# Cosine-gated MLP behind linear attention on one Trainium2 core: the second layer's product with seven half-size products instead of eight

## The chip, the cores and the metric

The kernel runs on one core of one Trainium2 chip. The metric is the device time of one execution in microseconds. Before the change the median of 3 runs is 312.84 us (312.84 to 312.94).

## The reference

The inputs are q, k and v of 8 batches, 8 heads, 576 positions and 64 values a head (float32), w_in (512 x 2048) and w_out (2048 x 512). Attention is linear: no softmax, but features phi and two products, normalised by a sum.

```
c, s = cos(pi/2 * pos/576), sin(pi/2 * pos/576)
phi(x) = concat(relu(x) * c, relu(x) * s)            # 64 -> 128 features
q_p, k_p = phi(q), phi(k)
kv  = k_p^T @ v            # per batch and head, 128 x 64
z   = sum of k_p over positions
num = q_p @ kv ;  den = q_p . z + 1e-6
attn = num / den
x = attn as (8*576 tokens, 512)
h = x @ w_in               # first layer, 4608 x 2048
g = h * cos(h)
out = g @ w_out            # second layer, 4608 x 512
```

## The kernel before

All products run in f16 with sums in float32. The 4608 tokens are cut into nine chunks of 512 (`SM`): chunks 0 to 7 are the first 512 positions' worth of a batch, and chunk 8 (`xR`) gathers the 64 tokens that each batch has left over. `NJT` = 16 is the number of 128-row blocks of the inner dimension 2048, `NCT` = 4 that of 512.

For a batch, `attention(b)` loads k, q and v, forms phi on DVE and ACT (`prep`, lines 235 and 238), casts v into `V1` (`cast_v`, two buffers, with a column of ones that makes z come out of the same product), forms kv on PE (`kv`, line 259), transposes q (`q_pe` on PE in the early batches, `q_dma` on the DMA queue later), forms numerator and denominator (`num`, lines 322 to 342) and transposes the normalised result (`x_pe` or `x_dma`) into `xT`.

`layer1(c)` makes h transposed, 128 inner values by 512 tokens at a time: 4 matmuls of 512 columns into one of three PSUM banks `M1` (line 425), or, for chunks 0 and 1, 8 matmuls of 256 columns (line 408). `gate` then takes cos on ACT as a sine with a bias (line 381), and DVE multiplies it with h into `gT` (line 383), which is f16, inner blocks by tokens, with two buffers for alternate chunks.

`layer2(c)` uses `gT` as the stationary operand: for each of four blocks of 128 tokens, 16 matmuls of 512 columns accumulate over the inner dimension into one of two banks `M2` (line 449). ACT copies the bank to `ost` (line 461; the last one is split between ACT and DVE, lines 464 and 467), and SP's queue stores it (line 472). In the steady part `layer2(c-1)` runs beside `layer1(c)`.

The order of the work is written by a planner (`Plan`). Each step names its engine, its assumed time, a due time, and the keys that it reads and writes. `run` simulates the five queues: at each point it takes, among all steps that are ready, the one that can start first, and of equal ones the one with the earlier due time, and this fixes every engine's program order. Due times come from `start[c]` and `width[c]`; periods are `TP` = 30 us apart in the planner's time. The engines then run their own lists in order and wait for each other by semaphores. Weights come over POOL's queue (lines 514 and 524), and the loads of batch 1 wait for a part of w_out (`hold_raw`, line 528).

Of the kernel before, what the change touches and what calls it, by code (L numbers as in the profile page):

```python
# [99 lines left out]
def kernel(  # L100
# [9 lines left out]
    nc = tc.nc  # L110
# [71 lines left out]
    pl = Plan()  # L182
    MM, MMH, MMA, MMT = 0.2157, 0.109, 0.031, 0.057

    T0, TW, TP = 17.0, 46.0, 30.0
    start = [T0, TW] + [TW + 14.0 + TP * n for n in range(NC)]
    width = [14.0, 14.0] + [TP] * NC

# [51 lines left out]
                op0=ALU.max, op1=ALU.mult), rd, wr)  # L240

    def cast_v(b, t, eng, due, hs=slice(0, H)):
        out_, in_ = V1[b % 2][:, t, hs, 0:D], raw["v"][:, hs, t, :]
        heads = range(H)[hs]
        rd, wr = hk("v", heads), [("V1", b % 2, t, h) for h in heads]
        f = len(heads) / H
        if eng == "ACT":
            act(0.2 + 0.37 * f, due, lambda: nc.scalar.activation(
                out=out_, in_=in_, func=AF.Copy), rd, wr)
        else:  # L250
            dve(0.09 + 0.28 * f, due, lambda: nc.vector.tensor_copy(  # L251
                out=out_, in_=in_), rd, wr)

    def kv(b, due, split=False):
        def mm(hb):
            for hh in range(HB):
                h = hb * HB + hh
                for t in range(NT + 1):
                    nc.tensor.matmul(  # L259
                        ATT[:, hb, hh * D1:(hh + 1) * D1],  # L260
                        lhsT=kp[:, t, h].rearrange("p g d -> p (g d)"),
                        rhs=V1[b % 2][:, t, h, :], start=(t == 0), stop=(t == NT))
        for hb in range(2):
            hs = range(hb * HB, (hb + 1) * HB)
            pe(HB * (NT + 1), MMA, due, lambda hb=hb: mm(hb),
               [("kp", t, g, h) for t in range(NT + 1) for g in range(2) for h in hs]
               + [("V1", b % 2, t, h) for t in range(NT + 1) for h in hs],
               [("ATT", hb)])
# [119 lines left out]
    def layer1(c):  # L388
        X = xT[c % 2] if c < B else xR
        xk = [("xT", c % 2, t) for t in range(NT)] if c < B else [("xR", i) for i in range(NT)]  # L390
        G = gT[c % 2]
        if c < 2:
            n = 0
            for quarter in range(4):
                for hf in range(2):
                    for jp in range(2):
                        j0 = quarter * 4 + jp * 2
                        m = m1n[0] % NM1
                        m1n[0] += 1
                        due = start[c] + n * width[c] / NJT  # L400
                        n += 1
                        ts = slice(hf * 2 * P, (hf + 1) * 2 * P)

                        def mm(m=m, j0=j0, ts=ts):
                            for jj in range(2):
                                j = j0 + jj
                                for cc in range(NCT):
                                    nc.tensor.matmul(  # L408
                                        M1[m][:, jj * 2 * P:(jj + 1) * 2 * P],
                                        lhsT=w_in_sb[:, cc, j * P:(j + 1) * P], rhs=X[:, cc, ts],  # L410
                                        start=(cc == 0), stop=(cc == NCT - 1))
                        pe(2 * NCT, MMH, due, mm, xk[2 * hf:2 * hf + 2] + [("w_in", quarter)],
                           [("M1", m)])
                        gate(M1[m], ("M1", m), G[:, j0:j0 + 2, ts],
                             [("g", c, j, t) for j in (j0, j0 + 1) for t in (2 * hf, 2 * hf + 1)],
                             due + 1.5)
            return
        for j in range(NJT):
            m = m1n[0] % NM1
            m1n[0] += 1  # L420
            due = start[c] + j * width[c] / NJT

            def mm(m=m, j=j):
                for cc in range(NCT):
                    nc.tensor.matmul(M1[m], lhsT=w_in_sb[:, cc, j * P:(j + 1) * P], rhs=X[:, cc, :],  # L425
                                     start=(cc == 0), stop=(cc == NCT - 1))
            pe(NCT, MM, due, mm, xk + [("w_in", j // 4)], [("M1", m)])
            gate(M1[m], ("M1", m), G[:, j, :], [("g", c % 2, j, t) for t in range(NT)], due + 1.5)
# [5 lines left out]

    on = [0]

    def layer2(c):
        G = gT[c % 2]
        NQ = 4
        for t in range(NT):  # L440
            m = m2n[0] % NM2
            m2n[0] += 1
            w0, ww = (start[c + 1], width[c + 1]) if 0 < c < B else (start[c] + width[c], 14.0)
            for jq in range(NQ):
                due = w0 + ((t + (jq + 1) / NQ) / NT) * ww * 0.97

                def mm(m=m, t=t, jq=jq):
                    for j in range(jq * NJT // NQ, (jq + 1) * NJT // NQ):
# [5 lines left out]
            last = c == NC - 1 and t == NT - 1  # L454
            if t % 2 == 0:
                o = on[0] % NO
                on[0] += 1
            O = ost[o]
            due += 1.0
            if not last:  # L460
                act(0.5, due, lambda O=O, t=t, m=m: nc.scalar.activation(  # L461
                    out=O[:, t % 2, :], in_=M2[m], func=AF.Copy), [("M2", m)], [("ost", o, t % 2, 0)])
            else:
                act(0.3, due, lambda O=O, t=t, m=m: nc.scalar.activation(
                    out=O[:, t % 2, 0:256], in_=M2[m][:, 0:256], func=AF.Copy),
                    [("M2", m)], [("ost", o, t % 2, 0)])
                dve(0.33, due, lambda O=O, t=t, m=m: nc.vector.tensor_copy(
                    out=O[:, t % 2, 256:512], in_=M2[m][:, 256:512]),
                    [("M2", m)], [("ost", o, t % 2, 1)])

            def put(dst, s, keys, q=nc.sync, eng="SP", nb=256.0):
                pl.add(eng, 0.65, 0, due + 1.0, lambda: q.dma_start(out=dst, in_=s), keys, [],
                       dma=(nb, 330.0))
            if c < B:
                if t % 2 == 1:
                    n = c % 2
                    five, four = rows(c)
                    keys = [("ost", o, 0, 0), ("ost", o, 1, 0)]
                    put(five[:, t - 1:t + 1, :], blocks(O, n), keys)
                    put(four[:, t - 1:t + 1, :], blocks(O, 1 - n), keys)  # L480
            else:
                for n in range(2):
                    five, _ = rows(2 * t + n)
                    if not last:
                        put(five[:, NT, :], blocks(O, n)[:, t % 2], [("ost", o, t % 2, 0)], nb=131.0)
                    else:
                        for f in range(2):
                            fs = slice(f * 256, (f + 1) * 256)
                            put(five[:, NT, fs], blocks(O, n)[:, t % 2, fs],
                                [("ost", o, t % 2, f)], *((nc.scalar, "ACT") if f == 0 else (nc.sync, "SP")), nb=65.0)  # L490


    def setup():
        for nm in "kqv":
            nc.vector.memset(raw[nm][:, :, NT, :], 0.0)
        nc.vector.memset(PIH, math.pi / 2.0)
        nc.scalar.dma_start(out=CS, in_=cs_dr.ap())
        nc.scalar.dma_start(out=IDENT, in_=ident_dr.ap())
        nc.scalar.activation(out=WARM, in_=PIH, func=AF.Sin)
        for n in range(2):  # L500
            nc.gpsimd.memset(V1[n][:, :, :, D], 1.0)

    wi = moe_w_in.rearrange("(c p) f -> p c f", p=P)
    wo = moe_w_out.rearrange("(j p) m -> p j m", p=P)
# [144 lines left out]
```

## Time and profile before

| what | value |
|---|---|
| median of 3 runs | 312.84 us (312.84 to 312.94) |
| the profiled execution's own time | 311.55 us |
| its span, first to last instruction | 309.8 us |
| busy: PE, DVE, ACT | 284.9, 183.0, 185.9 us |
| weight loads on PE (beside the matmuls) | 158.2 us, 2092 of them |
| moved by DMA | 51.91 MB |
| mean granted TensorE clock | 0.994 |

An engine's busy time is the time that it had an instruction in work. Matmuls are pipelined: each one's recorded length is a latency, and what a stream of them costs is told by the distance of their starts. PEld is the weight loads, which run beside the matmuls. In the groups of instructions a row reads line, engine, operation, output<-input, shapes, count | busy us, mean ns of one | idle time of the engine just before them and who ended it. In the order of time a row reads start, length (both in us), engine, line and so on, with the idle time ahead of it in brackets. In the windows, each engine's busy time and count follow the length of the window, then the granted clock, the DMA share and GB/s.

### The profile page before, as it was taken

How to read it: one execution, taken by the hardware profiler on the slowest of the kernel's cores; microseconds unless marked ns; L12 is line 12 of the kernel's file. 1: busy time of each engine (PE TensorE's matmuls, PEld its weight loads, DVE VectorE, ACT ScalarE, POOL GpSimd, SP SyncE). 2: the span in 40 equal slices, each digit the busy share in tenths (PEclk: the TensorE clock that was granted, in tenths of full speed). 3: DMA queues.
4: the chain of work that ended last, by engine and by line, in shares of the span. 5: the costliest groups of instructions: out<-in, count | busy, mean ns of one | idle time of the engine just before them, and what ended most of it. 6: DMA issues, size and time to landing. Idle time of an engine off the chain costs nothing.

```text
span 309.8 us, 5467 instructions
## 1 busy us (share of the span) xinstructions
PE 284.9 (92%) x2092; PEld 158.2 (51%) x2092; DVE 183.0 (59%) x402; ACT 185.9 (60%) x297; POOL 7.9 (3%) x19
## 2 busy tenths in 40 slices
PE   0468999689999999999999999999999999999994
PEld 0447856477864555455545554544444444444441
DVE  1667655979896973985587665733565434343300
ACT  1947759689986856944884586444544454555311
POOL 0331000000000000000000000000000000000000
PEclk9999999989999999999999999999999999999999
DMA  6899998995499998997999732960132010101121
GB/s 195 271 210 223 187 324 270 357 332 164 142 234 232 364 177 218 309 268 118 282 341 252 119 102 65 159 148 5 69 70 85 1 70 0 69 0 70 42 94 68
DMA packets 72218, 51.91 MB, mean 168 GB/s; under 512 B 40832, under 2 KB 69760, under 8 KB 72192
## 3 DMA queue, kind: packets, MB, share of 16 engines
q1 hardware_dynamic: 67520, 47.20, 55.8%
q0 software_dynamic: 4224, 4.19, 8.3%
q8 instruction: 16, 0.26, 0.3%
q10 hardware_dynamic: 448, 0.17, 0.2%
q14 instruction: 10, 0.08, 0.1%
HBM read 36.74 MB, written 9.44 MB: 149 GB/s over the span
## 4 chain that ended last, share of the span: by engine, by line
PE 85%; DVE 5%; ACT 4%; DMA 2%; issue 1%; SPq 0%; DVEq 0%; ACTq 0%
PE M L449 39%; PE M L425 31%; PE M L408 7%; PE ATT L259 3%; PE ATT L322 3%; DMA qm<-in_q_dram 2%; DVE x L342 2%; PE M L290 1%; ACT ch L381 1%; ACT kp L235 1%; ACT qp L235 1%; DVE V L251 1%; DVE qp L238 1%; PE TR L290 0%; PE TR L361 0%
## 5 line engine op out<-in xcount | busy, mean ns | idle before, releaser
L381 ACT ACTIVATE ch<-M,PIH 128x512 f32<-128x512 f32 x144 | 98.5, 692 | 80.4 <-PE M L425 60.6
L383 DVE TENSOR_TENSOR gT<-M,ch 128x512 f16<-128x512 f32 x144 | 98.3, 687 | 77.3 <-ACT ch L381 76.8
L449 PE MATMUL M<-w_out_sb,gT 128*128 128x512 f16 x576 | 142.6, 379 | 0.0
L425 PE MATMUL M<-xT,w_in_sb 128*128 128x512 f16 x384 | 96.9, 379 | 0.0
L449 PEld LDWEIGHTS <-gT 128*128 128x128 f16 x576 | 54.5, 98 | 60.5
L425 PEld LDWEIGHTS <-w_in_sb 128*128 128x128 f16 x448 | 43.3, 98 | 51.1
L408 PE MATMUL M<-xT,w_in_sb 128*128 128x256 f16 x256 | 30.2, 272 | 0.7 <-ACT xT L365 0.7
L235 ACT ACTIVATE kp<-km,CS 128x512 f16<-128x512 f32 x40 | 26.5, 719 | 6.5 <-DMA km<-in_k_dram 6.5
L461 ACT ACTIVATE ost<-M 128x512 f32<-128x512 f32 x35 | 20.7, 594 | 15.5 <-PE M L449 15.1
L235 ACT ACTIVATE qp<-qm,CS 128x512 f16<-128x512 f32 x39 | 26.4, 726 | 2.9 <-DMA qm<-in_q_dram 2.7
L408 PEld LDWEIGHTS <-w_in_sb 128*128 128x128 f16 x256 | 24.4, 98 | 3.6 <-issue 0.8
L238 DVE TENSOR_SCALAR kp<-km,CS 128x512 f16<-128x512 f32 x40 | 16.9, 480 | 14.3 <-DMA km<-in_k_dram 11.1
L342 DVE TENSOR_TENSOR x<-ATT,rec 128x512 f16<-128x512 f32 x30 | 20.6, 688 | 0.8
L238 DVE TENSOR_SCALAR qp<-qm,CS 128x512 f16<-128x512 f32 x41 | 18.3, 477 | 2.5 <-DMA qm<-in_q_dram 2.5
L322 PEld LDWEIGHTS <-qT 128*128 128x128 f16 x320 | 14.3, 98 | 6.7 <-issue 1.0
L290 PEld LDWEIGHTS <-qp 128*128 128x128 f16 x120 | 8.9, 111 | 15.2 <-ACT qp L235 12.2
L425 PE MATMUL M<-xR,w_in_sb 128*128 128x512 f16 x64 | 16.4, 379 | 0.0
L290 PE MATMUL M<-IDENT,qp 128*128 128x128 f16 x56 | 4.9, 259 | 12.2 <-ACT qp L235 12.2
L259 PE MATMUL ATT<-V,kp 128*128 128x65 f16 x320 | 13.3, 202 | 2.5 <-DVE x L342 1.7
L259 PEld LDWEIGHTS <-kp 128*128 128x128 f16 x320 | 12.6, 103 | 5.2 <-issue 2.7
L251 DVE CAST V<-vm 128x512 f16<-128x512 f32 (+1 forms) x42 | 14.0, 383 | 0.0
L322 PE MATMUL ATT<-kvz,qT 128*128 128x65 f16 x272 | 13.5, 194 | 0.0
(43 smaller groups left out, 76.6 us busy)
## 6 DMA issues: line engine op xcount, KB each, us to landing
out_dram<-ost SPq DMA_DIRECT2D x32, 256.0 KB, 2.6
km<-in_k_dram SPq DMA_DIRECT2D x8, 640.0 KB, 5.3
qm<-in_q_dram SPq DMA_DIRECT2D x8, 640.0 KB, 5.2
km<-in_k_dram SPq DMA_DIRECT2D x8, 512.0 KB, 6.2
qm<-in_q_dram SPq DMA_DIRECT2D x8, 512.0 KB, 6.2
vm<-in_v_dram SPq DMA_DIRECT2D x6, 640.0 KB, 7.1
vm<-in_v_dram SPq DMA_DIRECT2D x6, 512.0 KB, 7.7
w_in_sb<-in_moe_w_in_dram POOLq DMA_DIRECT2D x4, 512.0 KB, 9.4
```

Source lines behind the costliest of these rows:

```text
L235: act(0.2 + 0.37 * f, due, lambda: nc.scalar.activation(out=out_, in_=in_, func=AF.Relu, scale=sc), rd, wr)
L238: dve(0.09 + 0.28 * f, due, lambda: nc.vector.tensor_scalar(out=out_, in0=in_, scalar1=0.0, scalar2=sc, op0=ALU.max, op1=ALU.mult), rd, wr)
L251: dve(0.09 + 0.28 * f, due, lambda: nc.vector.tensor_copy(out=out_, in_=in_), rd, wr)
L259: nc.tensor.matmul(ATT[:, hb, hh * D1:(hh + 1) * D1], lhsT=kp[:, t, h].rearrange("p g d -> p (g d)"), rhs=V1[b % 2][:, t, h, :], start=(t ...
L322: nc.tensor.matmul(bank[hb][:, hh * D1:(hh + 1) * D1], lhsT=a[:, h, :], rhs=z[:, h, :], start=(i == 0), stop=(i == len(parts) - 1))
L342: dve(0.08 + 0.27 * k, due, lambda A=A, hs=hs, k=k: nc.vector.tensor_tensor(out=split(x16[n][:, hs, :], k), in0=A[:, :, :, 0:D], in1=split ...
L381: act(0.59, due, lambda: nc.scalar.activation(out=ch[c], in_=bank, func=AF.Sin, bias=PIH, scale=1.0), [key, "PIH"], [("ch", c)])
L383: dve(0.61, due, lambda: nc.vector.tensor_tensor(out=dst, in0=bank if len(dst.shape) == 2 else bank.rearrange("p (j s) -> p j s", j=dst.sh ...
L408: nc.tensor.matmul(M1[m][:, jj * 2 * P:(jj + 1) * 2 * P], lhsT=w_in_sb[:, cc, j * P:(j + 1) * P], rhs=X[:, cc, ts], start=(cc == 0), stop= ...
L425: nc.tensor.matmul(M1[m], lhsT=w_in_sb[:, cc, j * P:(j + 1) * P], rhs=X[:, cc, :], start=(cc == 0), stop=(cc == NCT - 1))
L449: nc.tensor.matmul(M2[m], lhsT=G[:, j, t * P:(t + 1) * P], rhs=w_out_sb[:, j, :], start=(j == 0), stop=(j == NJT - 1))
L461: act(0.5, due, lambda O=O, t=t, m=m: nc.scalar.activation(out=O[:, t % 2, :], in_=M2[m], func=AF.Copy), [("M2", m)], [("ost", o, t % 2, 0)])
```

## The change

The second layer of chunks 1 to 8 is done with one level of Strassen's scheme (Winograd's form: seven products). The operands are cut in halves: `gT` by tokens (`TH` = 256) and by inner blocks (`JH` = 8), `w_out` by inner blocks and by columns (`MH` = 256). With a11, a12, a21, a22 for `gT` (first index tokens, second inner half) and b11 to b22 for `w_out`, the sums and products are:

```
T1 = b12 - b11   T3 = b22 - b12   T2 = b22 - T1   T4 = b21 - T2      # once, w_out_sums
S3 = a11 - a21   S1 = a21 + a22 (in a21's place)   S2 = S1 - a11   S4 = a12 - S2 (in a12's place)
bank A : a11 b11 -> copy Y1 ; + S2 T2 -> copy U2 ; + S3 T3 -> c22 = bank + Z5 ; + a22 T4 -> c21
bank Bk: a12 b21 -> c11 = bank + Y1 ; new: S1 T1 -> copy Z5 ; + S4 b22 -> c12 = bank + U2
```

The products are issued in the order A, Bk, A, Bk, A, Bk, A. Each is 2 token blocks x 8 inner blocks of matmuls with 256 columns. Sums of `gT` are made on DVE in f16, in two halves of four inner blocks each; the four copies are on ACT, the three adds that end an output quarter on DVE. `layer1` now alternates between the two inner halves, so that the first halves of the sums can be made before its end. Batch 0 keeps the plain product as `layer2_plain(0)`. `V1` goes from two buffers to one, and `TP` from 30 to 28. A chunk's two output tiles `ost` are held from its first to its last product instead of being filled and stored one after the other.

```diff
-    V1 = [sb(f"V1_{n}", [P, NT + 1, H, D1]) for n in range(2)]
+    V1 = sb("V1", [P, NT + 1, H, D1])
+    JH, MH, TH = NJT // 2, Dm // 2, SM // 2
+    T1, T2, T3, T4 = [sb(f"T{n}", [P, JH, MH]) for n in range(1, 5)]
+    S2, S3 = [sb(f"S{n}", [P, JH, TH]) for n in (2, 3)]
+    Y1, U2, Z5 = [sb(nm, [P, 2, MH], F32) for nm in ("Y1", "U2", "Z5")]
...
-    T0, TW, TP = 17.0, 46.0, 30.0
+    T0, TW, TP = 17.0, 46.0, 28.0
...
-        for j in range(NJT):
+        for n in range(NJT):
+            j = n // 2 + (n % 2) * JH
             m = m1n[0] % NM1
             m1n[0] += 1
-            due = start[c] + j * width[c] / NJT
+            due = start[c] + n * width[c] / NJT
...
+    def store(c, h, o, due, fs=None):
+        O = ost[o]
+        keys = [("ost", o, f) for f in range(2)]
+        if c < B:
+            n = c % 2
+            five, four = rows(c)
+            put(due, five[:, 2 * h:2 * h + 2, :], blocks(O, n), keys)
+            put(due, four[:, 2 * h:2 * h + 2, :], blocks(O, 1 - n), keys)
+            return
+        for tt in range(2):
+            for n in range(2):
+                five, _ = rows(2 * (2 * h + tt) + n)
+                if fs is None:
+                    put(due, five[:, NT, :], blocks(O, n)[:, tt], keys, nb=131.0)
+                else:
+                    f = slice(fs * MH, (fs + 1) * MH)
+                    put(due, five[:, NT, f], blocks(O, n)[:, tt, f], [("ost", o, fs)],
+                        *((nc.scalar, "ACT") if n else (nc.sync, "SP")), nb=65.0)
...
+    def layer2_plain(c):
         G = gT[c % 2]
         NQ = 4
+        w0, ww = start[c] + width[c], 14.0
...
+    def w_out_sums():
+        W = w_out_sb
+        b11, b12 = W[:, 0:JH, 0:MH], W[:, 0:JH, MH:Dm]
+        b21, b22 = W[:, JH:NJT, 0:MH], W[:, JH:NJT, MH:Dm]
+        wk = [("w_out", g) for g in range(4)]
+
+        def tt(out_, a, b, op, rd, wr):
+            dve(1.14, start[1] - 2, lambda: nc.vector.tensor_tensor(
+                out=out_, in0=a, in1=b, op=op), rd, wr)
+        tt(T1, b12, b11, ALU.subtract, wk, ["T1"])
+        tt(T3, b22, b12, ALU.subtract, wk, ["T3"])
+        tt(T2, b22, T1, ALU.subtract, wk + ["T1"], ["T2"])
+        tt(T4, b21, T2, ALU.subtract, wk + ["T2"], ["T4"])
+
+    def layer2(c):
+
+        G, W = gT[c % 2], w_out_sb
+        lo, hi = slice(0, JH), slice(JH, NJT)
+        a11, a12 = G[:, lo, 0:TH], G[:, hi, 0:TH]
+        a21, a22 = G[:, lo, TH:SM], G[:, hi, TH:SM]
+        w0, ww = (start[c + 1], width[c + 1]) if c < B else (start[c] + width[c], 14.0)
+
+        def gk(hj, ht, js=range(JH)):
+            return [("g", c % 2, hj * JH + j, 2 * ht + t) for j in js for t in range(2)]
+        NG = 2
+        for q_ in range(NG):
+            js = range(q_ * JH // NG, (q_ + 1) * JH // NG)
+            sl = slice(js[0], js[-1] + 1)
+
+            def tt(out_, a, b, op, rd, wr, due, sl=sl):
+                dve(0.07 + 1.07 / NG, due, lambda: nc.vector.tensor_tensor(
+                    out=out_[:, sl], in0=a[:, sl], in1=b[:, sl], op=op), rd, wr)
+            tt(S3, a11, a21, ALU.subtract, gk(0, 0, js) + gk(0, 1, js), [("S3", q_)], w0 + 1)
+            tt(a21, a21, a22, ALU.add, gk(0, 1, js) + gk(1, 1, js), gk(0, 1, js), w0 + 1)
+            tt(S2, a21, a11, ALU.subtract, gk(0, 1, js) + gk(0, 0, js), [("S2", q_)], w0 + 1)
+        sk = {n: [(n, q_) for q_ in range(NG)] for n in ("S2", "S3")}
+        wk = [("w_out", g) for g in range(4)]
+        A, Bk = m2n[0] % NM2, (m2n[0] + 1) % NM2
+        m2n[0] += 2
+        order = iter(range(1, 8))
+
+        def product(bank, a, b, rd, first, last):
+            n = next(order)
+            for tt in range(2):
+                due = w0 + (n - 0.5 + 0.5 * tt) / 7 * ww * 0.97
+
+                def mm(tt=tt):
+                    for j in range(JH):
+                        nc.tensor.matmul(
+                            M2[bank][:, tt * MH:(tt + 1) * MH], lhsT=a[:, j, tt * P:(tt + 1) * P],
+                            rhs=b[:, j, :], start=(first and tt == 0 and j == 0),
+                            stop=(last and tt == 1 and j == JH - 1), skip_group_check=True)
+                pe(JH, MMH, due, mm, rd, [("M2", bank)])
+            return due
+
+        def view(bank):
+            return M2[bank].rearrange("p (t m) -> p t m", t=2)
+
+        def copy(dst, bank, dk, due):
+            act(0.5, due, lambda: nc.scalar.activation(out=dst, in_=view(bank), func=AF.Copy),
+                [("M2", bank)], dk)
+
+        def plus(dst, bank, other, ok, dk, due):
+            dve(0.61, due, lambda: nc.vector.tensor_tensor(
+                out=dst, in0=view(bank), in1=other, op=ALU.add), [("M2", bank), ok], dk)
+        ol, oh = on[0] % NO, (on[0] + 1) % NO
+        on[0] += 2
+        m0, m1 = slice(0, MH), slice(MH, Dm)
+        d = product(A, a11, W[:, lo, m0], gk(0, 0) + wk, True, False)
+        copy(Y1, A, ["Y1"], d + 0.5)
+        d = product(Bk, a12, W[:, hi, m0], gk(1, 0) + wk, True, True)
+        plus(ost[ol][:, :, m0], Bk, Y1, "Y1", [("ost", ol, 0)], d + 0.5)
+        for q_ in range(NG):
+            js = range(q_ * JH // NG, (q_ + 1) * JH // NG)
+            sl = slice(js[0], js[-1] + 1)
+            dve(0.07 + 1.07 / NG, d + 2.0, lambda sl=sl: nc.vector.tensor_tensor(
+                out=a12[:, sl], in0=a12[:, sl], in1=S2[:, sl], op=ALU.subtract),
+                gk(1, 0, js) + [("S2", q_)], gk(1, 0, js))
+        d = product(A, S2, T2, sk["S2"] + ["T2"], False, False)
+        copy(U2, A, ["U2"], d + 0.5)
+        d = product(Bk, a21, T1, gk(0, 1) + ["T1"], True, False)
+        copy(Z5, Bk, ["Z5"], d + 0.5)
+        d = product(A, S3, T3, sk["S3"] + ["T3"], False, False)
+        plus(ost[oh][:, :, m1], A, Z5, "Z5", [("ost", oh, 1)], d + 0.5)
+        d = product(Bk, a12, W[:, hi, m1], gk(1, 0) + wk, False, True)
+        plus(ost[ol][:, :, m1], Bk, U2, "U2", [("ost", ol, 1)], d + 0.5)
+        store(c, 0, ol, d + 1.5)
+        if c == B:
+            store(c, 1, oh, d + 1.0, 1)
+        d = product(A, a22, T4, gk(1, 1) + ["T4"], False, True)
+        if c < B:
+            copy(ost[oh][:, :, m0], A, [("ost", oh, 0)], d + 0.5)
+            store(c, 1, oh, d + 1.5)
+        else:
+            act(0.3, d, lambda: nc.scalar.activation(
+                out=ost[oh][:, 0, m0], in_=view(A)[:, 0], func=AF.Copy), [("M2", A)], [("ost", oh, 0)])
+            dve(0.33, d, lambda: nc.vector.tensor_copy(
+                out=ost[oh][:, 1, m0], in_=view(A)[:, 1]), [("M2", A)], [("ost", oh, 0)])
+            store(c, 1, oh, d + 1.0, 0)
...
     layer1(0)
     late_q0()
-    layer2(0)
+    layer2_plain(0)
     attention(1)
     layer1(1)
+    w_out_sums()
     for c in range(2, NC):
```

More of the change, by code (lines that the diff above doesn't have):

```diff
@@ L435, with put @@
     on = [0]
-    def layer2(c):
+    def put(due, dst, src_, keys, q=nc.sync, eng="SP", nb=256.0):
+        pl.add(eng, 0.65, 0, due, lambda: q.dma_start(out=dst, in_=src_), keys, [], dma=(nb, 330.0))
+    def store(c, h, o, due, fs=None):
[17 more added lines that the diff above has]
+    def layer2_plain(c):
         G = gT[c % 2]
         NQ = 4
+        w0, ww = start[c] + width[c], 14.0
         for t in range(NT):
@@ L442, in layer2 @@
             m2n[0] += 1
-            w0, ww = (start[c + 1], width[c + 1]) if 0 < c < B else (start[c] + width[c], 14.0)
             for jq in range(NQ):
-                due = w0 + ((t + (jq + 1) / NQ) / NT) * ww * 0.97
+                due = w0 + ((t + (jq + 1) / NQ) / NT) * ww
                 def mm(m=m, t=t, jq=jq):
@@ L457, in layer2 @@
                 on[0] += 1
[L458 to L490, printed above, removed]
+            act(0.5, due + 1.0, lambda O=ost[o], t=t, m=m: nc.scalar.activation(
+                out=O[:, t % 2, :], in_=M2[m], func=AF.Copy), [("M2", m)],
+                [("ost", o, f) for f in range(2)])
```

14 lines of the change are left out of this document (7 added, 7 removed).

## The prediction

> **What bounds the kernel now.** I read the page first (busy shares and the 40 slices), then the windows by stage, then the costliest groups with shapes kept apart, then the order of time on PE and on DVE where one of them is short.
>
> ```profile
> span 309.8 us, 5467 instructions
> PE 284.9 (92%) x2092; PEld 158.2 (51%) x2092; DVE 183.0 (59%) x402; ACT 185.9 (60%) x297; POOL 7.9 (3%) x19
> ...
> PE   0468999689999999999999999999999999999994
> ...
> DVE  1667655979896973985587665733565434343300
> ```
>
> PE is full from about 70 us to the end, and only there the work itself sets the time. DVE looks idle at 59%, but its digits are 7 to 9 in slices 7 to 16 and 3 to 4 in the last eight: the average hides two stages. The windows give the numbers (busy columns: PE, PEld, DVE, ACT, POOL):
>
> ```profile
> 50.00:60.00 10.00, 8.64 (x121) 5.97 (x119) 7.62 (x26) 8.90 (x16) 0.00 (x0) 1.00 1.04 357
> 60.00:70.00 10.00, 6.77 (x88) 6.11 (x88) 8.36 (x27) 6.87 (x13) 0.00 (x0) 0.83 1.00 329
> 80.00:90.00 10.00, 10.00 (x121) 7.96 (x119) 9.37 (x21) 8.84 (x16) 0.00 (x0) 1.00 0.69 156
> ...
> 118.00:209.00 91.00, 91.00 (x628) 45.22 (x625) 60.54 (x128) 58.97 (x95) 0.00 (x0) 1.00 0.81 199
> ...
> 240.00:270.00 30.00, 30.00 (x141) 13.62 (x140) 12.24 (x18) 14.07 (x21) 0.00 (x0) 1.00 0.09 36
> ```
>
> Three stages follow. Up to 70 us attention of batches 0 to 2 feeds PE, which has holes (4.6 us between 50 and 70). From 87 us to 290.7 us, seven periods hold layer 1 of chunk c and layer 2 of chunk c-1, with attention of a later batch in the first five; PE has no hole. In the end there is layer 2 of chunk 8 alone. Matmul time saved in the last two stages is time saved, as long as nothing else takes over.
>
> **PE: the products.** Chunks 1 to 8 each lose 64 matmuls of 512 columns and get 7 x 2 x 8 = 112 of 256 columns; batch 0 keeps its 64. The groups give only latencies, which overlap, so I take the pitch from two streams that run one after the other in the order of time on PE (start, length):
>
> ```profile
> 35.80 4.31 PE L408 MATMUL M<-xT,w_in_sb 128*128 128x256 f16 x38
> 39.95 7.93 PE L449 MATMUL M<-w_out_sb,gT 128*128 128x512 f16 x36
> 47.72 0.77 PE L259 MATMUL ATT<-V,kp 128*128 128x65 f16 x20
> ```
>
> (39.95 - 35.80) / 38 = 109.2 ns for 256 columns, each with a weight load of its own, and (47.72 - 39.95) / 36 = 215.8 ns for 512. So 512 x 215.8 ns = 110.5 us become 896 x 109.2 ns = 97.8 us: 12.6 us less PE work, 1.58 us a chunk. The extra 384 weight loads cost nothing by these rows, as the 256-column stream has one for each matmul too. Seven of the eight savings lie in the full stage, one in the tail.
>
> **DVE: the sums.** For each of the eight chunks the change adds eight half sums (S3, a21, S2 and a12, two halves each; 1024 f16 elements from two SBUF sources) and turns three of its bank evacuations into adds on DVE (512 f32 each, one source in PSUM). ACT has four copies of a chunk before and after. Nothing in this trace adds two f16 operands from SBUF. The nearest rows:
>
> ```profile
> L383 DVE TENSOR_TENSOR gT<-M,ch 128x512 f16<-128x512 f32 x144 | 98.3, 687 | 77.3 <-ACT ch L381 76.8
> L342 DVE TENSOR_TENSOR x<-M,rec 128x256 f16<-128x256 f32 x10 | 3.8, 417 | 0.1
> L296 DVE COPY qT<-M 128x1024 f16<-128x1024 f16 x5 | 3.4, 685 | 1.2 <-PE M L290 1.2
> ```
>
> The two two-source rows rise by 270 ns for 256 elements, one element per 1.05 ns, over a fixed 147 ns; at that rate a half sum takes 1.23 us. The one-source copy moves 1024 f16 elements in 685 ns, two per 1.05 ns, and that is the other end. I take 0.69 us, by the row with the same type and the same 1024 elements in and out, and keep 1.23 us as a rival. The page "VectorE: DVE Perf Modes" of the Trainium skill, section "The perf-mode tier table", says that a two-source operation on 16-bit SBUF data runs at two elements a cycle (1224 ns for 2048) and on fp32 or PSUM data at one (2293 ns); by it too the sum stands at the lower end, and no run here has shown it yet. The three adds cost what the gate costs, 0.69 us.
>
> So a chunk adds 8 x 0.69 + 3 x 0.69 = 7.6 us to DVE. What it has to fit into: between 118 and 209 us (window above) three batches of attention passed, told by the 40-matmul pieces of kv in the chain in order of time:
>
> ```profile
> 117.75 1.21 PE ATT L259 x40
> ...
> 208.69 1.21 PE ATT L259 x40
> ```
>
> That is 91.0 / 3 = 30.3 us of PE and 60.54 / 3 = 20.2 us of DVE a period. After: PE 30.3 - 1.6 = 28.7, DVE 20.2 + 7.6 = 27.8, or 97%. DVE goes from a third idle to nearly full. The two are so close that the point of change is worth working out: DVE passes PE when a half sum takes over (28.7 - 20.2 - 2.1) / 8 = 0.80 us, and eats the whole saving of a period at 1.0 us. Two things move the 97%. Operations that stand close take less than their duration, and operations that depend on each other take more; the order of time on DVE shows both:
>
> ```profile
> 129.99 0.76 DVE L251 CAST V<-vm 128x512 f16<-128x512 f32 x2
> 130.65 1.28 DVE L383 TENSOR_TENSOR gT<-M,ch 128x512 f16<-128x512 f32 x2
> ...
> 135.37 0.15 DVE L338 TENSOR_SCALAR den<-ATT 128x8 f32<-128x8 f32 x1
> 135.56 0.20 DVE L340 RECIPROCAL rec<-den 128x8 f32<-128x8 f32 x1
> 135.79 0.69 DVE L342 TENSOR_TENSOR x<-ATT,rec 128x512 f16<-128x512 f32 x1
> ```
>
> Two gates in 1.28 us are 0.60 apart (0.69 long); den, rec and x, each of which needs the one before, stand 0.03 to 0.04 us apart end to start. S3, a21 and S2 of one half form such a chain, so six of the eight sums cost about 0.73, and the gates fall from 0.69 towards 0.60. I set the two against each other and stay at 0.95 to 0.97.
>
> What waits behind the sums: the gates of layer 1, in DVE's order, and behind these the three M1 banks. Up to six sums in a row (4.4 us) can hold the gates at the start of a period. PE meanwhile has the first two products, which need no sum (16 x 2 x 109 ns = 3.5 us), and three layer 1 tiles (2.6 us): 6.1 us of cover. Evacuations have less. A product lasts 1.75 us, and its bank is taken again after one other product; an ACT copy begins 0.17 us after the last matmul and takes 0.60 (rows of the tail, below), so it is hidden with about 1 us over, and a DVE add is hidden as long as fewer than one and a half operations stand ahead of it, twice that where layer 1 tiles lie between. On SP the stores of a chunk wait for these adds, with q and x transposes behind them; the stores keep their number and size until the last chunk, which has a few more small ones, two of them on ACT's queue. A period 5% shorter raises the DMA share of 0.81 (window 118:209) to 0.85, with the same transfers.
>
> That PE stays full while DVE is at 94% is shown by 80:90 above. I charge 1.5 us for the full stage, between 0 and 5.5 us: the upper end takes 0.937 as the most that DVE can be filled, which makes a period (27.8 + 0.2) / 0.937 = 29.9 us, 1.1 us over PE, in five periods. I stay nearer to 0, because 0.937 is what that window had with PE full, not a limit that it ran into.
>
> **The sums of w_out.** Four operations of 2048 elements go before layer 1 of chunk 1: at two elements per 1.05 ns 4 x 1.23 = 4.9 us, at one 4 x 2.3 = 9.2 us. They need all of w_out, whose last part was issued at 24.0 us and lands 10.0 to 15.6 us later, so by 39.6 us at the latest. DVE in that stage, and under it the loads of w_out (two rows of the view of that tile):
>
> ```profile
> 40.87 0.69 DVE L383 TENSOR_TENSOR gT<-M,ch 128x512 f16<-128x512 f32 x1 [0.18 <-ACT ch L381]
> 44.28 2.07 DVE L238 TENSOR_SCALAR kp<-km,CS 128x512 f16<-128x512 f32 x5 [2.72 <-DMA km<-in_k_dram]
> 47.62 0.49 DVE L238 TENSOR_SCALAR qp<-qm,CS 128x512 f16<-128x512 f32 x1 [1.27 <-DMA qm<-in_q_dram]
> ...
> 54.56 1.28 DVE L238 TENSOR_SCALAR kp<-km,CS 128x512 f16<-128x512 f32 x3 [2.23 <-DMA km<-in_k_dram]
> ...
> L524 POOL DMA_DIRECT2D w_out_sb<-in_moe_w_out_dram x4: 745/755/770, 21.8 to 24.0; - x4
> DMA to landing us min/median/max: 10.0/12.7/15.6
> ```
>
> The idle time in front of these rows, 2.72 + 1.27 + 2.23 = 6.2 us, is DVE waiting for data, and the sums fit in it if the planner's order meets it. If they come after 56 us, they stand on the path: there PE waits for DVE (rows of PE; the third is the first 512-column matmul of layer 1, with which the full stage begins):
>
> ```profile
> 58.39 0.40 PE L361 MATMUL M<-IDENT,x 128*128 128x128 f16 x4 [1.25 <-DVE x L342]
> ...
> 62.28 2.36 PE L259 MATMUL ATT<-V,kp 128*128 128x65 f16 x40 [1.73 <-DVE x L342]
> ...
> 87.24 1.03 PE L425 MATMUL M<-xT,w_in_sb 128*128 128x512 f16 x4
> ```
>
> Between 0 and 4.9 us I take 1.0: the first gap of 2.72 us holds two of the four, the planner starts whatever can start first, and the other two push batch 1's preparations by a part of their length. V1 with one buffer costs nothing: kv at 117.75 is done 11 us before the next batch's casts at 129.99 (both rows above); were it late, the casts would wait, and the gates behind them.
>
> **The tail.** Layer 2 of chunk 8 starts in the order of time at
>
> ```profile
> 290.68 14.84 PE L449 MATMUL M<-w_out_sb,gT 128*128 128x512 f16 x68
> ...
> 291.60 0.69 DVE L383 TENSOR_TENSOR gT<-M,ch 128x512 f16<-128x512 f32 x1 [1.04 <-ACT ch L381]
> 291.75 0.60 ACT L461 ACTIVATE ost<-M 128x512 f32<-128x512 f32 x1 [0.17 <-PE M L449]
> ...
> 305.56 0.38 ACT L464 ACTIVATE ost<-M 128x256 f32<-128x256 f32 x1 [2.86 <-PE M L449]
> 305.97 1.21 ACTq L472 DMA_DIRECT2D out_dram<-ost  x2
> ```
>
> The last gate ends at 292.3. The second halves of a21 and S2 follow by 293.8. The third product, the first to need them, begins two products (3.5 us) after 290.7, at 294.2, and reaches the second half at 294.6: hidden by 0.8 us, and at 1.23 us a sum it would be late by about 0.5. After the last product stand the same half copies and the same four stores of 64 KB. The tail gives its full 1.58 us, already counted.
>
> **The sum.** The profiled execution took 311.55 us, 1.75 over its span of 309.8; the median of the runs, 312.84, is 1.29 above that. 309.8 - 12.6 + 1.0 + 1.5 = 299.7 us of span, and with 1.75 and 1.29 around it 302.7 us.
>
> **Rivals.** B: DVE's order. The 97% don't leave room for a fixed order; gates wait behind sums, M1 banks are freed late, PE gets holes in five periods. With the upper 5.5 us instead of 1.5: 306.7. For it, ACT in the trace already waits for DVE's gate:
>
> ```profile
> ACT ch L381 <- DVE gT L383: 15.3, 15, 1.3
> ```
>
> Against it, these waits did not reach PE, and DVE has slack again once attention is over (12.24 of 30 us in 240:270). C: the sums of w_out land in the chain behind 56 us and cost their full 4.9 instead of 1.0: 306.6. For it, their due time of 44 us lies behind all attention of batch 1 in the planner's order; against it, the 6.2 us of gaps. D, the other side: a sum of two f16 operands runs at one element per 1.05 ns as both two-source rows do. DVE then needs 20.2 + 8 x 1.23 + 2.1 = 32.1 us a period, 3.4 over PE, and sets the time in five of them: 17 us; the sums of w_out outgrow their gaps by 9.2 - 6.2 = 3.0. 300.2 + 17 + 3.0 = 320, slower by 2%. It decides from 1.0 us a half sum upward. For it stand the two rows; against it the f16 copy.
>
> **How the numbers follow.** A, the forecast: 0.62 (own range 299.5 to 305; the floor is 312.84 - 12.6 = 300.2, and 0.7 less if the new order fills some of the holes before 70 us). B 0.17, C 0.10, D 0.11. Predicted is A, 302.7. The range 299.5 to 309 holds A, B and C, and leaves out D and most of the case that B and C meet (310.6). About 0.2% is what a measurement of this kernel tells from no change. Faster: A, B and C less 0.03 for their meeting with a larger price, 0.86; D is slower, but 0.01 of it and those 0.03 may end near zero: same 0.04, slower 0.10.
>
> **What would show it.** In the changed kernel's profile: 896 matmuls of 256 columns at a pitch of 109 ns; the half sums at 0.69 us (above 0.80 B and D begin, at 1.23 D is right); DVE at nine tenths or more from 87 to 200 us with PE's windows still full; no wait of PE on DVE there above some tenths; the four w_out sums between 38 and 56 us, and the first 512-column layer 1 matmul, now at 87.2 us, within 1 us of that. The prediction is wrong if PE shows holes in front of layer 1 or the products released by DVE, or if that first matmul moves by several us.

## The result and the profile after

The changed kernel takes 303.33 us (median of 4 runs, 301.13 to 304.74) against 312.84; the ratio is 0.9694, with a 95% interval of 0.9634 to 0.9755. A second set gave 302.65 against 312.74, ratio 0.9683 (0.9661 to 0.9706). The forecast was 302.7.

First the page of the changed kernel: the span, the busy shares, and two of the rows of 40 slices.

```profile
span 302.7 us, 6349 instructions
PE 276.6 (91%) x2476; PEld 198.9 (66%) x2476; DVE 236.2 (78%) x494; ACT 186.0 (61%) x297; POOL 7.7 (3%) x18
...
PE   0488999858999999999999999999999999999993
...
DVE  1664779787989999989988999895699648666731
```

PE's work fell, its slices are as full as before from the tenth on, and from slice 11 to 27 DVE's digits are now 8 and 9 where they were 3 to 9. The costliest new groups of DVE, from the groups with shapes kept apart:

```profile
L520 DVE TENSOR_TENSOR S<-gT 128x1024 f16<-128x1024 f16 x32 | 21.7, 683 | 0.3
L497 DVE TENSOR_TENSOR T<-w_out_sb 128x2048 f16<-128x2048 f16 x2 | 2.4, 1215 | 0.0
L553 DVE TENSOR_TENSOR ost<-M,Y 128x512 f32<-128x512 f32 x8 | 5.5, 683 | 2.4 <-PE M L538 2.4
```

A half sum takes 0.68 us (1024 elements), a whole one 1.22 (2048): (1215 - 683) ns / 1024 is two elements per 1.04 ns, the lower end of the prediction's two. The windows of the changed kernel (PE, PEld, DVE, ACT, POOL busy, then clock, DMA share, GB/s):

```profile
90.00:120.00 30.00, 29.80 (x260) 20.74 (x259) 29.94 (x66) 20.47 (x34) 0.00 (x0) 1.00 0.95 218
120.00:150.00 30.00, 30.00 (x295) 21.10 (x293) 28.89 (x63) 21.54 (x35) 0.00 (x0) 1.00 1.02 261
240.00:270.00 30.00, 30.00 (x204) 19.77 (x202) 21.14 (x33) 15.17 (x23) 0.00 (x0) 1.00 0.09 36
```

DVE fills 29.94 of 30 us, and PE next to it still 29.80. The order of time on PE shows what a hole is and where the tail begins:

```profile
91.23 1.03 PE L430 MATMUL M<-xT,w_in_sb 128*128 128x512 f16 x4
...
283.29 1.04 PE L538 MATMUL M<-T,gT 128*128 128x256 f16 x8
285.01 3.65 PE L538 MATMUL M<-w_out_sb,gT 128*128 128x256 f16 x32 [0.69 <-ACT ost L549]
288.50 1.91 PE L538 MATMUL M<-T,S 128*128 128x256 f16 x16
```

32 matmuls of 256 columns take 288.50 - 285.01 = 3.49 us, 109.1 ns each: the pitch of the prediction. The first of them waits 0.69 us for an ACT copy.

Four moments divide every profile: the first 512-column matmul of layer 1, the first matmul of chunk 8's products, the last ACT copy, the end of the span. From the order of time of each kernel (b1, e0, e5 are described below):

| | first 512-column matmul | products of chunk 8 | last copy | end | between 1 and 2 | 2 and 3 | 3 and 4 |
|---|---|---|---|---|---|---|---|
| before | 87.24 | 290.68 | 305.56 | 309.8 | 203.44 | 14.88 | 4.24 |
| before, again (b1) | 88.23 | 291.68 | 306.56 | 310.8 | 203.45 | 14.88 | 4.24 |
| changed | 91.23 | 285.01 | 297.43 | 302.7 | 193.78 | 12.42 | 5.27 |
| changed, again (e0) | 89.44 | 283.22 | 295.64 | 300.9 | 193.78 | 12.42 | 5.26 |
| changed, mended (e5) | 89.33 | 281.89 | 294.32 | 298.7 | 192.56 | 12.43 | 4.38 |

The stretches repeat to 0.01 us. In these two pairs all that varies from one execution to the next lies in the first column. One caution for the kernel before: the row of 68 matmuls that starts at the second moment begins with the last four of chunk 7 (4 x 215.8 ns = 0.86 us), so chunk 8's own first matmul stands 0.86 us later there, at 291.54. The prediction too took 290.68 for the start of chunk 8.

### The profile page after: what moved, and what is told of

It reads as the page before. It is cut to its first block, busy times and chain, and to the rows that moved or that the text cites. A ratio compares the mean times of both kernels' runs of the same rounds, so it can differ in the third digit from the quotient of the medians.

```text
span 302.7 us, 6349 instructions
## 1 busy us (share of the span) xinstructions
PE 276.6 (91%) x2476; PEld 198.9 (66%) x2476; DVE 236.2 (78%) x494; ACT 186.0 (61%) x297; POOL 7.7 (3%) x18
## 4 chain that ended last, share of the span: by engine, by line
PE 81%; DMA 6%; ACT 4%; DVE 4%; issue 2%; SPq 1%; ACTq 0%; DVEq 0%
PE M L430 32%; PE M L538 31%; PE M L412 8%; PE ATT L263 4%; PE M L476 3%; DMA vm<-in_v_dram 3%; DMA qm<-in_q_dram 2%; PE ATT L326 2%; ACT ch L385 1%; DVE V L255 1%; PE M L294 1%; ACT kp L239 1%; ACT qp L239 1%; DVE x L346 1%; DMA out_dram<-ost 1%
## 5 line engine op out<-in xcount | busy, mean ns | idle before, releaser
L430 PE MATMUL M<-xT,w_in_sb 128*128 128x512 f16 x384 | 93.1, 379 | 0.0
L538 PEld LDWEIGHTS <-gT 128*128 128x128 f16 x640 | 61.6, 98 | 17.4 <-issue 1.2
L538 PE MATMUL M<-w_out_sb,gT 128*128 128x256 f16 x384 | 47.8, 272 | 0.9 <-ACT ost L549 0.9
L412 PE MATMUL M<-xT,w_in_sb 128*128 128x256 f16 x256 | 32.1, 282 | 0.9 <-ACT xT L369 0.8
L538 PE MATMUL M<-T,gT 128*128 128x256 f16 x256 | 32.8, 273 | 0.0
L538 PE MATMUL M<-T,S 128*128 128x256 f16 x256 | 32.4, 273 | 0.0
L538 PEld LDWEIGHTS <-S 128*128 128x128 f16 x256 | 24.8, 98 | 6.7
L520 DVE TENSOR_TENSOR S<-gT 128x1024 f16<-128x1024 f16 x32 | 21.7, 683 | 0.3
L326 PEld LDWEIGHTS <-qT 128*128 128x128 f16 x320 | 15.2, 101 | 4.4 <-issue 0.9
```

Source lines behind the costliest of these rows:

```text
L326: nc.tensor.matmul(bank[hb][:, hh * D1:(hh + 1) * D1], lhsT=a[:, h, :], rhs=z[:, h, :], start=(i == 0), stop=(i == len(parts) - 1))
L412: nc.tensor.matmul(M1[m][:, jj * 2 * P:(jj + 1) * 2 * P], lhsT=w_in_sb[:, cc, j * P:(j + 1) * P], rhs=X[:, cc, ts], start=(cc == 0), stop= ...
L520: dve(0.07 + 1.07 / NG, due, lambda: nc.vector.tensor_tensor(out=out_[:, sl], in0=a[:, sl], in1=b[:, sl], op=op), rd, wr)
L538: nc.tensor.matmul(M2[bank][:, tt * MH:(tt + 1) * MH], lhsT=a[:, j, tt * P:(tt + 1) * P], rhs=b[:, j, :], start=(first and tt == 0 and j = ...
```

## The experiments

**e0_again: the changed kernel once more.** No edit.

> The changed kernel as it is, for a second profile. Theory A (TensorE sets the time from the first 512-column matmul of layer 1 on, and the difference between executions lies ahead of it): the stretch from that matmul to the first matmul of chunk 8's products is again 193.8 us within 0.5, and where the total differs by 1 us or more, the start of that stretch differs by the same. Rival B (VectorE's fixed order is on the edge, and jitter in it makes the time vary): the stretch itself differs by 1 us or more, with holes of TensorE in it. Time 301 to 305 by both.

302.65 us; the stretch is 193.78 us again and the span 1.8 us shorter, with the first 512-column matmul 1.8 us earlier. Theory A holds: from there on the kernel repeats to 0.01 us, also where DVE is busy for 29.94 of 30 us.

**b1_before_again: the kernel before once more.** No edit.

> The kernel before, as it is, for a second profile. The five profiles of changed kernels all show the first 16 matmuls of layer 1 (22 to 27 us) at about 220 ns, the one of the kernel before at 109. If that is chance in the start of an execution and not of the change, this profile may show it too, and its span is then 310.5 to 312 with the whole difference ahead of 87 us; its stretch from the first 512-column matmul of layer 1 to the tail is 203.4 us as in the first profile, within 0.3. If the slow start belongs to the change, the start is at 109 ns again.

312.6 us (one execution), and the slow matmuls at the start are there too. PE in the second profile of the kernel before, where the first profile has 1.04 and 1.03 us for such a row of eight:

```profile
22.44 1.60 PE L408 MATMUL M<-xT,w_in_sb 128*128 128x256 f16 x8
24.07 1.90 PE L408 MATMUL M<-xT,w_in_sb 128*128 128x256 f16 x8
```

A matmul of the second row takes (25.76 - 24.07) / 8 = 211 ns and not 109. The windows from 23 to 26 us show the granted clock, the third number from the end, first in the first profile of before, then in this one:

```profile
23.00:26.00 3.00, 2.25 (x24) 1.79 (x23) 1.82 (x6) 2.20 (x4) 1.74 (x3) 1.00 1.18 249
```
```profile
23.00:26.00 3.00, 3.00 (x20) 2.26 (x19) 1.56 (x5) 0.93 (x2) 1.48 (x2) 0.50 1.18 247
```

So PE runs at half pace here, as the clock granted to it says. Seven of the eleven profiles show the doubled distance: this one, both of the changed kernel, e1, e2, e3 and e6. In six of them the granted clock falls to 0.50 between 23 and 25 us; in the first profile of the changed kernel it reads 1.00 although the matmuls are as far apart. It is chance in the start of an execution, of both kernels, and costs 1.1 to 1.5 us from the first matmul of layer 1 to the 40-matmul row that follows. So the first profile of before was one of the shorter executions, 1.0 us below this one, and the two profiles first shown overstate what the change loses ahead of 91 us. The page "TensorE: Matmul & The Clock Gate" of the Trainium skill, Part 1, describes a gate that halves TensorE's clock after idle time and opens after a busy window, and says that these windows run freely, whenever a kernel starts. The granted clock of 0.50 agrees, and so does its coming and going between executions of one program; that idle time sets it off here no run shows.

**e1_no_sums.** The eight half sums of a chunk are left out.

```diff
-            tt(S3, ...); tt(a21, ...); tt(S2, ...)      # and the two of a12
-        d = product(A, S2, T2, sk["S2"] + ["T2"], False, False)
+        d = product(A, a11, T2, gk(0, 0) + ["T2"], False, False)
-        d = product(A, S3, T3, sk["S3"] + ["T3"], False, False)
+        d = product(A, a12, T3, gk(1, 0) + ["T3"], False, False)
```

> Leaves out the eight half sums of a chunk on VectorE (S1 to S4); the products read the unsummed quarters instead, so TensorE's work is the same. Theory A (TensorE sets the time, VectorE is nearly full and hidden): 1 to 2 us faster than the changed kernel (301.3 to 302.3 beside 303.3), from the 0.9 us of holes and the sums between the gates before 91 us. Rival B (VectorE's order costs several us of the saving): 4 us faster or more, under 299.5.

303.17 us (301.96 to 304.08), ratio to before 0.9693 (0.9658 to 0.9727): no gain at all. The stretch is 284.31 - 90.17 = 194.14 us, 0.4 longer than with the sums: the planner's order differs, and PE waits twice for the copy of bank A (0.4 us between 90 and 284 us), where with the sums it waits once (0.2). Not even the 1 us of theory A came. The 34.5 us of DVE time that the sums take over the whole run (busy 236.2 with them, 201.7 without, in the two pages) are wholly hidden. That is 0.54 us for each of the 64, not 0.69: in a dense stream the beginning of one operation lies over the end of another (in the changed kernel two half sums that stand close take 1.28 us, 0.60 apart and 0.68 long).

```profile
PE 275.1 (91%) x2476; PEld 197.5 (66%) x2476; DVE 236.2 (78%) x494; ACT 185.9 (62%) x297; POOL 7.7 (3%) x18
```
```profile
PE 274.6 (91%) x2476; PEld 196.9 (65%) x2476; DVE 201.7 (67%) x430; ACT 185.9 (62%) x297; POOL 7.7 (3%) x18
```

(The first row is of e0_again, the second of e1_no_sums.)

**e2_four_extra and e6_eight_extra.** Four or eight further half sums a chunk, into a tile that nobody reads.

```diff
             tt(S2, a21, a11, ALU.subtract, ...)
+            for x in range(2):            # range(4) in e6; this stands in each of the two halves
+                dve(0.07 + 1.07 / NG, w0 + 1, lambda sl=sl: nc.vector.tensor_tensor(
+                    out=XS, in0=a11[:, sl], in1=a22[:, sl], op=ALU.add), ..., ["XS"])
```

> Adds four more half sums a chunk (same size, into a tile that nobody reads), so 12 instead of 8, 2.4 to 2.7 us of VectorE a chunk: as if a half sum took about 1.0 us. By the prediction's count VectorE then needs about 30.3 us a period against 28.7 of TensorE and sets the time in the five periods with attention: 8 us slower than the changed kernel, 308 to 314, near the kernel before. If VectorE has slack that the count missed (operations that stand close take 0.60 and not 0.69 us, and attention can slip into the last two periods): 1 to 3 us slower, 304 to 306.5.

> Eight extra half sums a chunk and not four: 16 in all. With four, the stretch grew by 1.7 us and VectorE was at 29.6 to 30.0 of 30 us from 90 to 210 us. If VectorE is now the limit there, each further sum costs its full 0.55 to 0.60 us in the five periods with attention: 4 x 5 x 0.6 = 12 us more than with four, 314 to 318. If work still slips into the last two periods (25.2 and 23.3 of 30 us in use with four), less: 307 to 313. If VectorE is no limit at all: 304.5 to 306.

Four: 304.45 us, ratio 0.9731 (0.9707 to 0.9755), stretch 285.26 - 89.82 = 195.44. Eight: 311.08, ratio 0.9937 (0.9916 to 0.9958), stretch 292.88 - 90.25 = 202.63. So the first four cost 1.7 us of the stretch and the next four 7.2. The count at 0.69 us a sum, by which four extra would bring the kernel back to 308 or more, fell; both runs came out in the range of their second expectation. The edge is there, but some four sums a chunk further out. One window each over the five periods with attention, of e0_again, of e2 and of e6:

```profile
90.00:210.00 120.00, 119.80 (x1074) 82.19 (x1072) 111.86 (x236) 81.51 (x131) 0.00 (x0) 1.00 0.90 209
```
```profile
90.00:210.00 120.00, 119.48 (x1068) 81.56 (x1067) 119.39 (x254) 81.03 (x129) 0.00 (x0) 1.00 0.85 201
```
```profile
90.00:210.00 120.00, 114.47 (x993) 76.67 (x992) 118.97 (x252) 79.08 (x125) 0.00 (x0) 1.00 0.82 194
```

With four extra DVE goes from 93% to 99.5% of the window, and PE is busy for 0.3 us less. With eight extra DVE takes no more (118.97 us), and PE gets the holes:

```profile
PEld L543 <- DVE S L521: 2.1, 4, 0.9
PE M L543 <- ACT ost L554: 1.6, 3, 0.7
PE M L543 <- ACT U L554: 1.5, 1, 1.5
PE M L543 <- DVE S L521: 1.1, 2, 0.6
```

(Waits of PE in e6 between 90 and 282 us. In e0_again the only wait of PE that names another engine there is "PE M L538 <- ACT ost L549: 0.2, 1, 0.2".)

**e3_no_wsums.** The sums of w_out are left out, the products read its quarters.

```diff
-    w_out_sums()
-        d = product(A, S2, T2, ...)        # and so on for T1, T3, T4
+        d = product(A, S2, W[:, hi, m1], ...)
```

> Leaves out the four sums of w_out (the products read its unsummed quarters). Theory A: they ran in VectorE's gaps between 42.8 and 50 us: no change, within 0.7 us of the changed kernel. Rival C (they are in the chain before the full stage): 2 to 4.9 us faster.

302.76 us (301.85 to 304.72), ratio 0.969 (0.965 to 0.973): no change that the medians show, though with this spread they can't tell 1 us from nothing. The rows can. In the changed kernel three of the sums lie between 42.8 and 46.8 us, where DVE would wait for k, and the fourth behind the five preparations of k:

```profile
42.79 1.22 DVE L497 TENSOR_TENSOR T<-w_out_sb 128x2048 f16<-128x2048 f16 x1
43.92 0.68 DVE L387 TENSOR_TENSOR gT<-M,ch 128x512 f16<-128x512 f32 x1
44.52 1.22 DVE L497 TENSOR_TENSOR T<-w_out_sb 128x2048 f16<-128x2048 f16 x1
45.66 1.22 DVE L497 TENSOR_TENSOR T<-w_out_sb,T 128x2048 f16<-128x2048 f16 x1
46.79 2.06 DVE L242 TENSOR_SCALAR kp<-km,CS 128x512 f16<-128x512 f32 x5
48.77 1.22 DVE L497 TENSOR_TENSOR T<-w_out_sb,T 128x2048 f16<-128x2048 f16 x1
```

PE needs 7.77 us from the 36-matmul row of batch 0's layer 2 to the first kv matmul with the sums (42.14 to 49.91), without them (41.01 to 48.78) and in the kernel before (39.95 to 47.72). The rows of PE that follow stay the same distance apart up to 59 us. Behind that, e3's profile gains 0.7 us on e0's, of which 0.4 are a shorter wait ahead of the 40 matmuls of kv (1.74 and 2.12 us). In the two profiles of the changed kernel alone that wait is 2.12 and 2.90 us, as v's load comes earlier or later (DVE waits 0.26 and 1.04 us for it), so it tells nothing of the sums. The rest falls among rows at half the granted clock (0.50 from 64 to 66 us in both). Rival C is out.

**e4_plan_only: three edits of the change alone.** The kernel before with TP 28, layer 1 alternating between the halves, and one V1.

```diff
-    T0, TW, TP = 17.0, 46.0, 30.0
+    T0, TW, TP = 17.0, 46.0, 28.0
-        for j in range(NJT):
+        for n in range(NJT):
+            j = n // 2 + (n % 2) * (NJT // 2)
-    V1 = [sb(f"V1_{n}", [P, NT + 1, H, D1]) for n in range(2)]
+    V1 = sb("V1", [P, NT + 1, H, D1])
```

> The kernel before with three edits of the change alone: TP 28, layer 1 alternating between the inner halves, V1 with one buffer; the second layer is plain. Theory A (the gain is TensorE's saved matmul time, the planner's edits are neutral): 312.8 within 0.8. Rival (a part of the loss ahead of 91 us comes from the planner's new due times or V1's single buffer): 1 to 3 us slower, with the first 512-column matmul at 88.5 us or later.

313.43 us against 313.15, ratio 1.0009 (0.9984 to 1.0035), and the stretch is 291.85 - 88.40 = 203.45 us, as before. These edits don't bring the gain and cost nothing in the stretch. Ahead of it the profile is 1.16 us behind the first one of before (88.40 against 87.24), both with the fast matmuls at the start; the interval of the ratio reaches 1.1 us too, so a cost there, some tenths up to 1 us, is not excluded.

**e5_tail: two mends.** The banks change places from chunk to chunk, and half of chunk 8's 128 KB stores go through POOL's queue.

```diff
-        m2n[0] += 2
+        m2n[0] += 3
-                    put(due, five[:, NT, :], blocks(O, n)[:, tt], keys, nb=131.0)
+                    put(due, five[:, NT, :], blocks(O, n)[:, tt], keys,
+                        *((nc.gpsimd, "POOL") if n else (nc.sync, "SP")), nb=131.0)
```

> The changed kernel with two edits: bank A and Bk change places from chunk to chunk, so that the first product of a chunk doesn't take the bank that the last product of the chunk before has just filled; and half of the four 128 KB stores of chunk 8 go through GpSimd's queue and not SyncE's. If both readings are right: the hole of 0.69 us ahead of the last chunk's products is gone, and the end from the last copy on takes 4.2 to 4.6 us and not 5.3; 1.2 to 1.7 us faster than the changed kernel, 301.0 to 301.6 beside 302.65 to 303.3. If SyncE's queue isn't what holds the last stores: only the hole, 0.7.

300.6 us (299.83 to 300.94), ratio to before 0.9598 (0.957 to 0.9626): 2.0 to 2.7 us better than the changed kernel and a little better than expected. Both edits were run together, but the table keeps their parts apart: the stretch is 1.22 us shorter, more than the hole of 0.69, and the end 0.88. What the first mend removed is seen in PE's order of time, where the products of chunk 8 now follow without a wait (0.87 us after the row before, where the changed kernel has 285.01 - 283.29 = 1.72):

```profile
281.02 1.04 PE L539 MATMUL M<-T,gT 128*128 128x256 f16 x8
281.89 3.66 PE L539 MATMUL M<-w_out_sb,gT 128*128 128x256 f16 x32
```

The second is seen in the queues' rows, first of the kernel before, then of the changed kernel and of e5 (start, length from the first issue to the end of the last):

```profile
305.56 0.38 ACT L464 ACTIVATE ost<-M 128x256 f32<-128x256 f32 x1 [2.86 <-PE M L449]
...
306.43 1.12 SPq L472 DMA_DIRECT2D out_dram<-ost  x2
```
```profile
294.72 5.36 SPq L443 DMA_DIRECT2D out_dram<-ost  x8
...
297.43 0.39 ACT L584 ACTIVATE ost<-M 128x256 f32<-128x256 f32 x1 [4.64 <-DMA out_dram<-ost]
```
```profile
291.60 4.25 SPq L443 DMA_DIRECT2D out_dram<-ost  x6
...
293.86 1.11 POOL L443 DMA_DIRECT2D out_dram<-ost  x2 [256.97 <-issue]
294.32 0.38 ACT L585 ACTIVATE ost<-M 128x256 f32<-128x256 f32 x1 [4.64 <-DMA out_dram<-ost]
```

In the changed kernel SP issued eight stores in 5.36 us, the last six of them in 3.67 (from 296.41 on, 0.61 each), and the last two were issued behind the others until 300.08, 2.65 us after the start of the last copy. Before, that was 1.99 us (307.55 less 305.56), and with six in the row it is 1.53. From the last issue to the end of the span it is 2.3, 2.6 and 2.9 us in the three kernels. (The brackets of the last two copies name a store, but PE's last row ends at 297.40 and 294.28, some hundredths ahead of them: the copies follow PE.)

**e7_tail_tp30.** e5 with TP 30.

> The kernel of e5_tail with TP 30 instead of 28 in the planner's due times. If the engines' order hardly depends on it, since the planner starts whatever can start first: 300.6 within 0.8, and the stretch from the first 512-column matmul to chunk 8's products 192.6 us within 0.5. If the shorter period of the planner is a part of the gain: the stretch grows by 1 us or more, as gates and products with later due times fall behind attention on VectorE.

301.01 us (300.6 to 301.31), ratio 0.9622 (0.9606 to 0.9638), stretch 281.68 - 89.39 = 192.29, 0.3 us shorter than e5's. TP is no part of the gain.

## Why the prediction was right, step by step

The forecast of 302.7 stands beside 303.33 and 302.65. It was right in mechanism and in its largest term, and two smaller terms were off in opposite directions, so that part of the agreement is luck. I compare e0_again with b1, since both had the slow matmuls at the start (in brackets, the kernel before counted from chunk 8's own first matmul):

| | e0 less b1, us | predicted |
|---|---|---|
| up to the first 512-column matmul | +1.2, of which 0.6 is work moved ahead of it and 0.4 chance | +1.0 (w_out's sums) |
| the stretch | -9.67 (-10.53) | -9.5 (seven chunks' saving less 1.5) |
| tail to the last copy | -2.46 (-1.60) | -1.6 |
| end | +1.02 | 0 |
| span | -9.9 | -10.1 |

The 0.4 us stand there already at the first matmul of layer 1 (22.87 against 22.44): e0's half pace began earlier, with a granted clock of 0.62 from 18 to 22 us where b1 has 1.00.

**PE's saving, 12.6 us: right.** Stretch and tail shrank by 12.13 us. Of that 0.6 is a half of one kv (20 matmuls) that now stands ahead of the stretch, and against it stand 1.2 us by which e0's stretch is longer than that of e5, which has no holes: 12.13 - 0.6 + 1.2 = 12.7. In e5 the sum closes: 448 matmuls at 215.8 ns, 768 at 109.2 and 388 small ones at 31 ns make 192.6 us, and the stretch is 192.56. (The counts are those of PE's groups in that stretch; 31 ns is what the same sum leaves for the 408 small ones before: 203.44 less 884 x 215.8 ns.) The 384 additional weight loads cost nothing.

```profile
L430 PE MATMUL M<-xT,w_in_sb 128*128 128x512 f16 x384 | 93.2, 379 | 0.0
L539 PE MATMUL M<-w_out_sb,gT 128*128 128x256 f16 x320 | 40.2, 273 | 0.0
L539 PE MATMUL M<-T,gT 128*128 128x256 f16 x224 | 29.0, 273 | 0.0
L539 PE MATMUL M<-T,S 128*128 128x256 f16 x224 | 28.5, 273 | 0.0
L430 PE MATMUL M<-xR,w_in_sb 128*128 128x512 f16 x64 | 16.1, 379 | 0.0
L326 PE MATMUL ATT<-kvz,qT 128*128 128x65 f16 x208 | 10.8, 194 | 0.0
L263 PE MATMUL ATT<-V,kp 128*128 128x65 f16 x180 | 6.4, 193 | 0.0
```

**The full stage, 1.5 us: the size right, the cause wrong.** e0's stretch is 1.2 us longer than e5's. But it isn't DVE's order: without any sums (e1) the stretch is no shorter, and the hole ahead of chunk 8 is the same 0.69 us. It is the hand-over of bank A: in the prediction every bank "is taken again after one other product", and between chunks that is not so. The seventh product fills A, and the first of the next chunk takes A. In the periods layer 1 tiles cover most of it; ahead of chunk 8 nothing does, and PE stood idle for 0.69 us there, and for 0.20 once before (116.22 in e0). An idle time counts from the modelled end of the last matmul; counted by starts, as the streams are, the first costs 1.72 - 8 x 0.109 = 0.85 us and the second (16 small matmuls, then 0.85 us to the next start) 0.35, together the 1.2 us.

**DVE's price, 0.69 us a half sum: too high.** A sum alone takes 0.68, but adds 0.54 (e1), 0.48 (e2) and 0.55 us (from e2 to e6) to DVE's busy time. The count of 97% came out at 93% between 90 and 210 us (111.86 of 120). The point of change of 0.80 us a sum was well placed, if a sum is priced at what it adds (a reading of these runs, not a run of its own): over the prediction's 64 sums, the DVE time of e2's sums makes (34.5 + 15.4) / 64 = 0.78 us each, just below it, and cost 1.7 us; that of e6 makes 67.4 / 64 = 1.05, well above it, and cost 8.9, most of the gain. Rival B is out at this load; rival D's premise is out by the rows of L520. Its mechanism, DVE as the bound, is what e6 shows.

**The sums of w_out, 1.0 us: too high.** They delayed nothing on PE up to 59 us (e3); the gap in front of k's preparations took three of them, and the fourth delayed nothing that PE waited for. The first 512-column matmul did come 1.2 us later, as forecast, but for other reasons (the table): that is the luck.

**The tail: "the same half copies and the same four stores", the step that failed.** The stores behind the last copy are the same, but the queue ahead of them is not. Before, chunk 8's outputs were stored as they came, a product of 3.45 us (16 x 215.8 ns) apart; now a whole output tile comes out with the sixth product, and its four 128 KB stores and two halves stand on SP in front of the last two. I counted the stores and not what they queue behind. The end grew by 1.0 us: 0.7 is the queue (the last issue ends 2.65 and not 1.99 us after the copy's start), the rest lies behind the last issue and stays open.

## What to carry to other kernels

Where one engine is full, count its saved work by the pitch of streams in the trace: 12.6 us of matmul time came as 12.7, though VectorE went from 59% to 78% busy. Price work that is added to a dense in-order engine by what it adds to the busy time (here 0.54 us for an operation that takes 0.68 alone), and find the edge by adding more of the same: four extra sums a chunk cost 1.7 us, eight 8.9. Look last at the hand-overs that the average hides, the bank between two chunks and the store queue ahead of the last store; mending these two took about 303 us to 300.6.

## What was not expected of the hardware

The start varies between executions of one program: 16 matmuls of 256 columns run at about 109 or, all or some of them, at about 212 ns from 22 to 27 us, in profiles of both kernels. In the two profiles of the changed kernel, which are 1.8 us apart, 1.0 stands there by the 40-matmul row and 0.8 is a later load of v (DVE waits 1.04 and 0.26 us for it at 60 to 63 us), while the stretch behind repeats to 0.01 us. Every profile also has a second piece of 2 us or more at a granted clock of 0.50, around 65 us, beside PE's waits for DVE (1.7 to 2.9 us long). So a single profile of each of two kernels can be 2 us apart for no reason of theirs, and a difference between two versions is better read from the stretches than from the spans.
